# Three reorderings in a turn of a recurrent-attention and routed feed-forward kernel: products by u behind the row fetch, sums split the same way in every turn, one score copy moved

## The chip, the cores and the metric

The kernel runs on one core of one Trainium2 chip. A core has TensorE (PE, matrix products; its weight loads are listed as PEld), VectorE (DVE), ScalarE (ACT), GpSimd (POOL) and SyncE (SP, which issues most of the DMAs here). Each engine works through its own queue of instructions in order; engines wait for each other by semaphores. The metric is the device time of one execution in microseconds (us); less is better. Times of a kernel are medians of several runs.

## What is computed

The first part is a recurrent attention (RWKV6) over 4 batches, 8 heads, 768 positions and 48 values a head, with a state of 48 x 48 for each head:

```python
for t in range(S):
    cur = np.einsum('bhd,bhe->bhde', u[None] * kt, vt)
    y[:, :, t] = np.einsum('bhd,bhde->bhe', rt, state + cur)
    state = wt[:, :, :, None] * state + np.einsum('bhd,bhe->bhde', kt, vt)
```

The term of a position with itself, r . (u * k) times v, doesn't need the state: it is one number for each position and head, times v. The second part takes the result x (768 rows of 384 for each batch), scores each row, and puts the 128 best rows of a batch through a feed-forward block:

```python
scores = np.einsum('bsd,d->bs', x, w_gate)
for b in range(B):
    top_idx = np.argpartition(-scores[b], capacity)[:capacity]
    xe = x[b, top_idx]
    h = np.maximum(xe @ w1, 0.0)
    ye = h @ w2
    g = 1.0 / (1.0 + np.exp(-scores[b, top_idx]))
    out[b, top_idx] = x[b, top_idx] + g[:, None] * ye
```

All data is 32-bit; w1 is 384 x 1024, w2 is 1024 x 384.

## The kernel before

The 768 positions of a batch are cut into 6 chunks of 128, so there are 24 chunks. A chunk's attention is computed in matrix form: running products of the decays w (two scans on VectorE), r and k scaled by them (`R`, `K`), a masked score product, the product with v, and a state that is carried from chunk to chunk.

The order of the work is written out by hand. `turn(i)` is called for i from -2 to 24, and it works on several chunks at once, in different stages: the inputs of chunks i + 1 and i + 2 are transposed and scaled, the scores and outputs of chunk i are computed, the output rows of chunk i - 1 are turned back, written and scored, and the scores of chunk i - 2 are compared with those of its batch. The order in which `turn` calls the stages is the order of the instructions in each engine's queue. A later instruction of a queue can't overtake an earlier one that waits.

The stages that matter here, with their lines:

- **The term of a position with itself.** `own_products` (L367, GpSimd) multiplies r and k of chunk i + 1; `own_weights` (L370, GpSimd) multiplies that by u; one turn later `own_values` (L378, ScalarE) sums each of the 8 heads in an ACTIVATE with an accumulator, and `own_results` (L387, mostly GpSimd) multiplies v by the sums. `own_values` is called at two places of a turn: a first group of heads early, the rest after the rows of the chunk before have been copied. `FIRST` is 5 heads. From turn 9 on (`LATE` is 9) the first group is empty when no feed-forward work is waiting at that moment; this happens in turn 9 only.
- **State and rows.** `back` (L420, ScalarE copies `kt` out of a PSUM bank of a pool of two), `rows_back` (L470, ScalarE copies `x` out; in the last two turns L468 on VectorE), `rows_out` (L476 on GpSimd adds the term above, L477 on SP stores the rows), `row_products` (L481, GpSimd multiplies the rows by the gate weights into `scr`) and `row_sums` (L486, ScalarE sums `scr` to the scores). From turn 9 on `row_sums` stands ahead of the copies `yt` (L459) in ScalarE's queue; in turns up to 8 it stands behind the copy (L456).
- **Comparing scores.** `compared` transposes a chunk's scores on TensorE (L552, `ps_e`) and compares them on VectorE (L554 against the chunks before, L558 within the chunk); `kept` (L568, ScalarE) copies the transposed scores into `every` for the chunks that follow. `kept` can run only when L558 is done.
- **Choosing rows.** When a batch's 6 chunks are scored, `mixture` runs as a generator through the turns that follow: ranks (L587 on TensorE, L594 and L595 on VectorE), six picks (L605, VectorE, 16-bit), an index product (L614 on TensorE) and `idx` (L620, VectorE), and the fetch of the chosen rows by an indirect DMA from GpSimd's queue (L629); a turn later the rows are transposed (L638, `ps_x`) and copied to `xeT` (L640, ScalarE). Each `mix(place=...)` in `turn` runs the generator on by one piece if that piece belongs there. The picks of the first batch come at the end of turn 7, its fetch in turn 8; for the second and third batch picks and fetch are in turns 14 and 20; the last batch's are after the last turn.
- **Feed-forward.** `forward` is a generator too: 8 groups of 3 products (L674, `ps_h`), with a copy `hid` (L679, ScalarE) after each 4 groups, then 8 products (L686, `ps_f`), then the gated result (L693) and a scattered store (L696). `fed_in_turn` runs a few pieces of it at two places of a turn.

Of the kernel before, what the change touches and what calls it, by code (L numbers as in the profile page):

```python
# [37 lines left out]
def kernel(  # L38
# [43 lines left out]
    B, H, S, D = r.shape  # L82
# [11 lines left out]
    LATE = S // L + 3  # L94

    FIRST = H * 5 // 8
# [21 lines left out]
    N = len(chunks)  # L118
# [43 lines left out]
    def loads(n):  # L162
        load(v_bufs, v, n - 3)
        load(k_bufs, k, n - 1)
        load(r_bufs, r, n - 1)
        load(w_bufs, w, n)
# [19 lines left out]
    def load_weights(n):  # L186
        while n > 0 and weights:
            to, src = weights.pop(0)
            nc.sync.dma_start(out=to, in_=src)
            n -= 1  # L190
# [67 lines left out]
    def warm(n):  # L258

        ps = psM.tile([L, 512], FP32, tag="m", name="ps_n")  # L260
        for _ in range(n):
            nc.tensor.matmul(
                ps, nothing.to_broadcast([L, L]), nothing.to_broadcast([L, 512]),
                start=True, stop=True,
            )

    def spread(to, row):

        ps = psM.tile([L, C], FP32, tag="m", name="ps_b")
        nc.tensor.matmul(ps, one_row, row, start=True, stop=True)  # L270
        nc.scalar.copy(out=to, in_=ps)
# [46 lines left out]
    def check_sums():  # L318

        above = setup.tile([L, 1], FP32)  # L320
        nc.vector.tensor_reduce(out=above, in_=guard, axis=AX.X, op=ALU.add)
        below = setup.tile([L, 1], FP32)
        junk = setup.tile([L, N * HP], FP32)
        nc.vector.tensor_scalar(
            out=junk, in0=alls.rearrange("p n j -> p (n j)"), scalar1=float(LOW ** L),
            scalar2=None, op0=ALU.is_lt, op1=ALU.add, accum_out=below,
        )
        return above, below
# [377 lines left out]
    mixing, picked, feed, ended, sums = [], [], [], [], []  # L706

    def step(f, n, *more):
        if 0 <= n < N:
            f(work.setdefault(n, dict(n=n)), *more)  # L710

    def mix(n=1, place=None):


        while n > 0 and mixing:
            if place is not None and mixing[0][1] not in (None, place):
                return
            try:
                mixing[0][1] = next(mixing[0][0])
                n -= 1  # L720
            except StopIteration:
                mixing.pop(0)

    def fed(n, on=True):

        while n > 0:
            if not feed:
                if not picked:
                    return
                feed.append((picked[0][0], forward(*picked.pop(0))))  # L730
            try:
                last = next(feed[0][1])
                n -= 1
                if last and not on:
                    return
            except StopIteration:
                feed.pop(0)

    def fed_in_turn(n, few):

        kept = (feed or picked) and (feed or picked)[0][0] == B - 2
        fed(few if kept else n, on=False)
# [6 lines left out]
    def turn(i):  # L749
        soon = i >= N - 1  # L750
        step(first_left, i + 1)
        if i < 1:
            step(scaled_aside, i + 1, "K", "right")
        step(own_products, i + 1)
        if i <= LATE:
            step(scores, i)

        first = FIRST if i < LATE or feed or picked else 0
        step(own_values, i, range(first))
        step(carry, i - 1, work.get(i))  # L760
        if i > 0:
            step(scaled, i + 1, "K", "right")
        mix(place="picks")
        if i >= 0:
            step(own_weights, i + 1)
        if soon:
            step(masked, i)
        if i == N - 1:
            sums.extend(check_sums())
        if i < N:  # L770
            step(compared, i - 2)
        if i < LATE:
            step(kept, i - 2)
        step(back, i)
        if LATE <= i < N:
            step(kept, i - 2)
        step(rows_back, i - 1, soon)
        mix(place="half")
        if not soon:
            step(masked, i)  # L780
        step(rows_out, i - 1, soon)
        step(row_scores_soon if soon else row_products, i - 1)
        step(own_values, i, range(first, H))
        step(own_results, i)
        fed_in_turn(PIECES // 2, 2 if i >= N - 1 else 1)
        mix(place="sum")
        step(inputs_t, i + 1, "R", r_bufs)
        if i == -1:
            spread(wg_bc, wg_row)
        step(scaled, i + 1, "R", "left")  # L790
        step(decays_t, i + 2)
        mix(place="mid")
        if i == -2:
            warm(2)
        step(range_check, i + 2)
        if i >= LATE and not soon:
            step(row_sums, i - 1)
        if i == -1:
            spread(u_bc.rearrange("p h d -> p (h d)"), u_row)
            step(own_weights, i + 1)  # L800
        step(carry_products, i)
        step(outputs_t, i)
        if i >= LATE:
            step(scores, i + 1)
        step(inputs_t, i + 2, "K", k_bufs)
        if i == -2:
            warm(1)
        if 0 <= i - 2 < N - 1 and chunks[i - 2][1] == NCH - 1:
            mixing.append([mixture(chunks[i - 2][0]), "ranks"])
        mix(place="ranks")  # L810
        fed_in_turn(PIECES - PIECES // 2, 1 if i == N - 1 else 0)
        if i == N - 1:
            step(compared, i - 1)
            step(kept, i - 1)
        if i < LATE and not soon:
            step(row_sums, i - 1)
        step(scans, i + 2)
        if i < LATE:
            mix(place="picks")
        mix(place="end")  # L820
        if i > -2:
            loads(i + 5)
        if i in WEIGHT_TURNS:
            load_weights(1)

    with tc.manual_schedule():
        warm(6)
        for i in range(-2, N + 1):
            turn(i)

        ended.append(True)
        mix(1000)
        mixing.append([mixture(B - 1), "picks"])
        step(compared, N - 1)
        step(kept, N - 1)
        fed(1)
        mix(2)
        wide = checked(sums)
        fed(1)
        mix()  # L840
        fed(NFC - 2)
        mix(2)
        fed(2)
        mix(1000)
        fed(1000)
        outside = nc.values_load(wide, min_val=0, max_val=1)
# [73 lines left out]
```

## Time and profile before

| | |
|---|---|
| median of 3 runs | 200.09 us (199.82 to 200.36) |
| the profiled execution's own time | 199.46 us |
| its span, first to last instruction | 197.8 us |
| mean granted TensorE clock | 0.995 |
| sums of own values, L378, ScalarE | 192 ACTIVATEs of 241 ns, each with an accumulator read of 197 ns |
| product by u, L370, GpSimd | 24 of 1002 ns |
| product by gate weights, L481, GpSimd | 22 of 1004 ns |
| picks, L605, VectorE | 24 of 301 ns (240 to 1036) |
| copy of scores, L568, ScalarE | 20 of 267 ns |
| fetch of rows, L629, GpSimd | 4 of 1096 ns; 3.3 us from issue to landing |

How to read the profile: in a list of groups each line gives source line, engine, operation, output and inputs, shapes and count, then busy time, mean duration and the idle time of the engine just before, with what ended it. An ACTIVATE and its accumulator read overlap, so the eight sums of a chunk follow each other every 0.23 us. A line of the list of waits gives the engine and line that waited, what it waited for, and the us in total, the times and the longest. In a timeline each line is: start, duration, engine, line, operation, and in brackets the idle time before it. The chain of waits is followed back from the last instruction; a wait on several semaphores is put down to the one that came last. Turn 8 lies at about 57 to 64 us, turn 9 at 64 to 72, turn 14 at 101 to 108, turn 20 at 144 to 152, turn 23 at 166 to 170, and the feed-forward of the last batch ends the span.

### The profile page before, as it was taken

What the parts mean: (1) busy time and instruction counts of PE and PEld (TensorE: products, weight loads), DVE (VectorE), ACT (ScalarE), POOL (GpSimd) and SP (SyncE); (2) the same over time, 40 slices, a digit from 0 to 9 for tenths busy, and PEclk for the clock granted to TensorE, in tenths of its full rate; (3) what the DMA queues carried; (4) which work ended last, traced back from release to release, by engine and by line L of the source; (5) the groups of instructions that cost most, each with busy time, mean ns of one, the idle gap of its engine ahead of it and who ended that gap; (6) DMA issues with size and microseconds to landing.
All of it is one profiled execution on the core that took longest, in us unless ns stands there. A gap on an engine that the chain in (4) does not pass through costs nothing.

```text
span 197.8 us, 7207 instructions
## 1 busy us (share of the span) xinstructions
PE 183.4 (93%) x2674; PEld 149.9 (76%) x2675; DVE 160.3 (81%) x348; ACT 129.4 (65%) x668; POOL 139.4 (70%) x186
## 2 busy tenths in 40 slices
PE   7898999989799989999999999999999999899970
PEld 3477787867686779898788798897878798777830
DVE  6999899999999978998989888999989886751010
ACT  4588999998974777669556768777666766410300
POOL 8699899995886995587658799579649796122201
PEclk9999999999999999999999999999999999999998
DMA  7999999989999999999894796897954131111101
GB/s 111 164 163 152 172 197 173 254 172 161 224 204 252 222 193 243 226 219 197 160 207 104 145 206 129 110 180 138 150 100 122 46 77 45 40 45 41 40 8 45
DMA packets 105390, 28.86 MB, mean 146 GB/s; under 512 B 100482, under 2 KB 104580, under 8 KB 105348
## 3 DMA queue, kind: packets, MB, share of 16 engines
q1 hardware_dynamic: 104304, 26.65, 74.7%
q0 software_dynamic: 512, 1.57, 2.6%
q8 instruction: 23, 0.38, 0.9%
q14 instruction: 19, 0.16, 0.3%
q10 hardware_dynamic: 532, 0.10, 0.3%
HBM read 22.81 MB, written 5.51 MB: 143 GB/s over the span
## 4 chain that ended last, share of the span: by engine, by line
PE 65%; ACT 11%; DMA 8%; SPq 5%; DVE 5%; issue 2%; POOL 0%; POOLq 0%; DVEq 0%
PE ps_h L674 11%; PE ps_f L686 11%; PE ps_s L402 9%; PE ps_t L277 7%; SPq L157 5%; PE ps_t L284 5%; PE ps_kv L507 4%; PE ps_yt_y L442 4%; PE ps_yt_y L450 3%; PE ps_w L277 3%; DMA v_buf<-in_v_dram 3%; PE ps_yt_k L442 3%; DMA k_buf<-in_k_dram 3%; ACT rk L378 3%; DMA r_buf<-in_r_dram 2%; ACT vo L391 2%
## 5 line engine op out<-in xcount | busy, mean ns | idle before, releaser
L378 ACT ACTIVATE rk<-rk 128x48 f32<-128x48 f32 x192 | 44.4, 241 | 0.1
L378 ACT ACTIVATION_READ_ACCUMULATOR rk<-rk 128x1 f32 x192 | 37.8, 197 | 0.0
L476 POOL TENSOR_TENSOR x<-x,vo 128x384 f32<-128x384 f32 x22 | 22.1, 1005 | 17.3 <-ACT x L470 17.1
L308 DVE TENSOR_TENSOR_SCAN left<-ps_w,from_left 128x511 f32<-128x511 f32 x24 | 30.7, 1281 | 0.9
L410 DVE TENSOR_TENSOR sc<-ps_s,before_f 128x1024 f32<-128x1024 f32 x24 | 29.2, 1218 | 1.4 <-PE ps_s L402 1.4
L297 DVE TENSOR_TENSOR_SCAN right_buf<-ps_w,from_right 128x511 f32<-128x511 f32 x24 | 29.1, 1211 | 1.0 <-PE ps_w L277 1.0
L402 PE MATMUL ps_s<-R,K 64*64 64x128 f32 x768 | 25.9, 272 | 1.7 <-ACT yt L456 0.9
L674 PE MATMUL ps_h<-xeT,w 128*128 128x128 f32 x192 | 25.0, 278 | 1.2 <-ACT hid L679 1.2
L674 PEld LDWEIGHTS ps_h<-xeT,w 128*128 128x128 f32 x192 | 22.9, 192 | 2.4 <-ACT hid L679 1.9
L370 POOL TENSOR_TENSOR rk<-rk,u_bc 128x384 f32<-128x384 f32 x24 | 24.1, 1002 | 1.0 <-DVE alls L303 0.5
L402 PEld LDWEIGHTS ps_s<-R,K 64*64 64x64 f32 x768 | 21.4, 133 | 4.1 <-ACT yt L456 3.3
L367 POOL TENSOR_TENSOR rk<-r_buf,k_buf 128x384 f32<-128x384 f32 x24 | 24.1, 1006 | 0.5 <-DMA r_buf<-in_r_dram 0.4
L686 PE MATMUL ps_f<-w,hid 128*128 128x384 f32 x64 | 23.5, 495 | 0.0
L481 POOL TENSOR_TENSOR scr<-x,wg_bc 128x384 f32<-128x384 f32 x22 | 22.1, 1004 | 1.7
L387 POOL TENSOR_TENSOR vo<-v_buf,own 128x384 f32<-128x384 f32 (+1 forms) x24 | 17.7, 737 | 3.4 <-ACT rk L378 3.4
L420 ACT COPY kt<-ps_t 128x384 f32<-128x384 f32 x20 | 9.6, 480 | 15.4 <-PE ps_t L284 15.3
L355 DVE TENSOR_TENSOR R<-ps_t,left 128x512 f32<-128x512 f32 x24 | 16.4, 685 | 3.1 <-issue 2.2
L486 ACT ACTIVATE scr<-scr 128x384 f32<-128x384 f32 x22 | 11.5, 525 | 9.9 <-POOL scr L481 9.7
L355 DVE TENSOR_TENSOR K<-ps_t,right_buf 128x512 f32<-128x512 f32 x22 | 15.0, 682 | 2.6 <-PE ps_t L277 1.9
L277 PE MATMUL ps_t<-ident,k_buf 128*128 128x128 f32 x96 | 15.7, 286 | 0.2 <-DMA k_buf<-in_k_dram 0.2
L277 PE MATMUL ps_t<-ident,r_buf 128*128 128x128 f32 x96 | 14.7, 275 | 1.1 <-DVE K L355 0.4
L277 PE MATMUL ps_w<-ident,w_buf 128*128 128x128 f32 x96 | 15.1, 281 | 0.6 <-ACT every L568 0.4
(131 smaller groups left out, 404.7 us busy)
## 6 DMA issues: line engine op xcount, KB each, us to landing
k_buf<-in_k_dram SPq DMA_DIRECT2D x24, 192.0 KB, 5.3
r_buf<-in_r_dram SPq DMA_DIRECT2D x24, 192.0 KB, 5.4
v_buf<-in_v_dram SPq DMA_DIRECT2D x24, 192.0 KB, 4.3
out_dram<-x SPq DMA_DIRECT2D x24, 192.0 KB, 3.8
w_buf<-in_w_dram SPq DMA_DIRECT2D x23, 192.0 KB, 4.5
w<-in_moe_w_dram SPq DMA_DIRECT2D x3, 512.0 KB, 5.7
w<-in_moe_w_dram SPq DMA_DIRECT2D x4, 384.0 KB, 5.5
w_buf<-in_w_dram ACTq DMA_DIRECT2D x1, 96.0 KB, 3.4
```

The source lines that it names most:

```text
L277: nc.tensor.transpose(ps[:, j, :], src(j), ident)
L297: nc.vector.tensor_tensor_scan(out=flat[:, W - 2::-1], data0=wt[:, W - 1:0:-1], data1=from_right.rearrange("p j t -> p (j t)")[:, W - 2::- ...
L308: nc.vector.tensor_tensor_scan(out=left.rearrange("p j t -> p (j t)")[:, 1:W], data0=wt[:, 0:W - 1], data1=start.rearrange("p j t -> p (j ...
L355: nc.vector.tensor_mul(out, t.pop(name + "t"), t.pop(by))
L367: nc.gpsimd.tensor_mul(rk, r_bufs[n % NBUF][:, :, 0:D], k_bufs[n % NBUF][:, :, 0:D])
L370: nc.gpsimd.tensor_mul(t["rk"], t["rk"], u_bc)
L378: nc.scalar.activation(out=rk[:, h, :], in_=rk[:, h, :], func=AF.Copy, accum_out=o[:, h:h + 1])
L402: nc.tensor.matmul(ps[half(c), q, j, :], t["K"][half(q), j, half(c)], t["R"][half(q), j, :], start=True, stop=True,)
L410: nc.vector.tensor_mul(t["sc"].rearrange("p q j t -> p (q j) t"), ps.rearrange("p q j t -> p (q j) t"), _heads(before_f, 2 * HP),)
L476: nc.gpsimd.tensor_add(x, x, t.pop("vo").rearrange("p h d -> p (h d)"))
L674: nc.tensor.matmul(ps[:, q, :], w1[:, dc, (f0 + q) * L:(f0 + q + 1) * L], xeT[:, dc, :], start=(dc == 0), stop=(dc == NDC - 1),)
L686: nc.tensor.matmul(ps, hid[:, fc, :], w2[:, fc, :], start=(fc == 0), stop=(fc == NFC - 1))
```

## The change

Only the order of calls in `turn` is changed; no instruction is added or removed.

- The early group of `own_values` is five heads in every turn (before, it was empty in turn 9).
- `own_weights` for the next chunk is called behind `mix(place="half")`, that is, behind the fetch on GpSimd in the turns that have one (8, 14 and 20), instead of behind `mix(place="picks")`. In the other turns nothing on GpSimd lies between the two places.
- In turn 23 (i == N - 1, the first of those called `soon`) `kept` of chunk 21 is called behind `own_results` and the first feed-forward piece, instead of behind `back`. On ScalarE this puts the copy behind the last three sums and behind `hid`. In turn 24 `kept` isn't called at this place, before or after.

```diff
-        first = FIRST if i < LATE or feed or picked else 0
-        step(own_values, i, range(first))
+        step(own_values, i, range(FIRST))
         step(carry, i - 1, work.get(i))
         if i > 0:
             step(scaled, i + 1, "K", "right")
         mix(place="picks")
-        if i >= 0:
-            step(own_weights, i + 1)
         if soon:
             step(masked, i)
...
-        if i < LATE:
+        if i < LATE and not soon:
             step(kept, i - 2)
         step(back, i)
-        if LATE <= i < N:
+        if i >= LATE and not soon:
             step(kept, i - 2)
         step(rows_back, i - 1, soon)
         mix(place="half")
+
+        if i >= 0:
+            step(own_weights, i + 1)
         if not soon:
             step(masked, i)
         step(rows_out, i - 1, soon)
         step(row_scores_soon if soon else row_products, i - 1)
-        step(own_values, i, range(first, H))
+        step(own_values, i, range(FIRST, H))
         step(own_results, i)
         fed_in_turn(PIECES // 2, 2 if i >= N - 1 else 1)
+        if i == N - 1:
+            step(kept, i - 2)
         mix(place="sum")
```

The functions called are unchanged.

## The prediction

> **What bounds the kernel now.** I read the page first, then the chain of waits in order of time, then the waits of the stretches that the diff touches, and last the timeline of the engines concerned. The page's engine shares, and the shares of the chain that ended last:
>
> ```profile
> PE 183.4 (93%) x2674; PEld 149.9 (76%) x2675; DVE 160.3 (81%) x348; ACT 129.4 (65%) x668; POOL 139.4 (70%) x186
> ...
> PE 65%; ACT 11%; DMA 8%; SPq 5%; DVE 5%; issue 2%; POOL 0%; POOLq 0%; DVEq 0%
> ```
>
> TensorE is the bound nearly everywhere; GpSimd holds none of the chain. So an edit on the other engines pays only where the chain leaves TensorE. The chain in order of time (start, us, what) shows two such places that the diff touches:
>
> ```profile
> 58.02 2.12 DVE pick L605 x6
> 60.13 0.61 DVE K L355
> 60.79 0.57 PE ps_t L277 x4
> ...
> 67.30 0.48 ACT x L470
> 67.78 0.93 ACT rk L378 x9
> 68.71 0.87 ACT rk L378 x7
> 69.58 0.37 ACT xeT L640
> 70.00 0.44 PE ps_yt_y L442 x4
> ...
> 168.95 0.68 ACT rk L378 x6
> 169.63 0.49 ACT hid L679
> 170.17 0.94 PE ps_h L674 x6
> ```
>
> From 72 to 166 us the chain is TensorE almost without a gap. (It also runs through input DMAs before 67.30; the copy there starts back to back on ScalarE, so I don't believe that link.) The waits in 57 to 72 us (turns 8 and 9), then in 166 to 172 us (turn 23):
>
> ```profile
> ACT kt L420 <- PE ps_t L284: 1.1, 1, 1.1
> ...
> PE ps_yt_y L442 <- ACT xeT L640: 0.9, 1, 0.9
> ```
>
> ```profile
> ACT every L568 <- DVE ahead L558: 2.3, 2, 1.3
> ...
> PE ps_h L674 <- ACT hid L679: 0.8, 1, 0.8
> ```
>
> TensorE stands 0.86 us (timeline) for the copy `xeT`, because eight sums L378 precede it, while ScalarE stood 1.07 us idle just before `kt`. In turn 23 it stands 0.84 us for `hid`, queued behind a copy `every` that waits 1.29 us for VectorE. Then the timeline of VectorE, GpSimd and ScalarE around the fetches:
>
> ```profile
> 58.02 2.12 DVE L605 TENSOR_SCALAR pick<-slots,rank 128x128 bf16<-128x128 bf16 x6
> 58.60 0.99 POOL L370 TENSOR_TENSOR rk<-rk,u_bc 128x384 f32<-128x384 f32 x1
> ...
> 61.42 1.24 POOL L629 DMA_INDIRECT xe<-out_dram,idx  x1 [1.83 <-DVE idx L620]
> ...
> 107.66 0.52 ACT L486 ACTIVATE scr<-scr 128x384 f32<-128x384 f32 x1 [1.91 <-POOL scr L481]
> ...
> 110.92 0.48 ACT L420 COPY kt<-ps_t 128x384 f32<-128x384 f32 x1 [0.89 <-PE ps_t L284]
> ```
>
> The six picks take 2.12 us in turn 8, but 1.21 in turns 14 and 20 and 1.07 in the tail. One of the six alone took 1036 ns (median 243), and it lies over L370. The fetch waits for `idx`, not for L370.
>
> **What the Trainium skill says.** "SBUF — State Buffer", section "Who interferes with whom": VectorE and GpSimd share one port pair as an exclusive lock; a VectorE instruction in a two-port mode and a GpSimd instruction block each other for the whole instruction. "VectorE: DVE Perf Modes", section "What auto-detection actually checks": a single source and destination of 16 bits in SBUF get the mode that uses both ports; that is the pick. The trace agrees: the pick beside L370 took 1036 ns, the one beside L527 505, those beside nothing 242. "Perfetto Trace Analysis", section "GPSIMD Engine Instruction", says to take GpSimd times from start-to-start spacing, so I use 0.96 us for L370 (66.96 to 67.92), not its 1.00.
>
> **The change part by part.** The order of instructions on TensorE, VectorE and SP is unchanged. On GpSimd only three pairs swap (L370 behind L629, turns 8, 14, 20); elsewhere nothing lies between the two places. On ScalarE the sums split as 5 + 3 in turn 9 alone, and one copy moves in turn 23.
>
> *Turn 8.* The third pick falls from 1036 to 242 ns: -0.79. `K` follows (end 60.73 to 59.94), the transposes of r (TensorE stood 0.42 us for `K`), `idx`, `sc`, `yt`: TensorE is 0.8 ahead at about 64. On GpSimd the fetch starts at 60.63, L370 follows (+0.96), so the row product `scr` ends at 64.91 against 64.78: 0.13 later than before, not 0.8 earlier. ScalarE's row sum L486 waits for it and ends near 65.55; TensorE's score transpose L552 waits for that (65.73 against 65.86). Most of the lead is gone here: -0.14.
>
> *Turn 9.* The five sums follow L316, 65.56 to 66.70 (5 x 0.228). `kt` was ready to start at 66.42 and starts at 66.70 against 66.58: the idle time of 1.07 covers nearly all of the sums, 0.12 shows. The r transposes need `kt`'s bank (67.24 against 67.12). Behind the copies only three sums are left (67.63 to 68.31). `ps_x` ends at 68.6, so `xeT` starts at 68.66 against 69.48, and TensorE's L442 at 69.2 against 70.00: **-0.80**. What is late next is TensorE itself: ps_kv ends at 69.2. GpSimd's `scr` of turn 9 ends at 70.13, its row sum at 70.8, just before `yt` can start (70.9). So of the two gains (0.79 and 0.86) the added GpSimd time swallows about one. Bounds: -0.3 if `scr` or `kt` is 0.5 later than I put them; -1.2 if the score isn't in the way. The TensorE-bound turns carry the lead on; inputs k and r of a chunk are issued about two turns ahead of use and land in 5.3 us, so I see no DMA that eats it.
>
> *Turns 14 and 20.* The fetch keeps its time: `idx` waits for TensorE's `ps_i`. The first pick loses its 0.14 of blocking, which nothing waits for. L370 now stands ahead of L476, L481 and L387: `scr` 0.95 late (107.63 to 108.58), so on ScalarE the row sum, both `yt` copies, L316 and five sums are 0.95 late, and `kt`, which waited 0.89 (0.87 in turn 20), starts up to 0.08 late. SP's output store and the loads of v, k, r, w queued behind it go 0.96 later too, with landing margins of microseconds; GpSimd itself recovers in its next idle time (1.22 and 1.21 us before L476). Cost 0.00 to 0.10 each, taken 0.05: **+0.10**. If the cover were gone it would be 0.95 each. Where L370 now lies, VectorE runs `R` and a scan, each with one operand in PSUM, so no new blocking: 0.
>
> *Turn 23.* ScalarE runs all eight sums in one piece, 166.15 to 167.97; `ps_h` ended at 167.63, so `hid` runs to 168.56. The copy still waits until 168.69 and delays nothing (`yt` can't start before 169.35). TensorE's second half L674 follows L450 at 169.33 instead of 170.17: -0.84. But the two score rounds behind it pass through VectorE: the second L558 starts at 170.59, when L554 ends, instead of 171.25; x L468, score L494 and the third L552 move by the same 0.66, and so do ranks, picks, fetch and the last feed-forward, an unbroken chain. **-0.66**, bounds -0.84 and -0.3.
>
> Sum: -0.80 + 0.10 - 0.66 = -1.36. The profiled execution took 199.46 us (span 197.8 and 1.66 around it), giving 198.10. It lies 0.63 below the median of 200.09; the same difference from the median gives **198.7 us**.
>
> **The rivals.** Differences within 0.3% (0.6 us) can't be told from none with this kernel.
>
> *Turns 8 and 9 give nothing:* the port lock stays busy, or the late row product on GpSimd holds ScalarE another 0.7 us. For it: 0.65 of the 0.79 is already lost at the score. Against: the 0.86 us that `xeT` costs has its own cause, eight sums ahead of it. -0.56: 199.5.
>
> *The moved copy gives nothing:* the lead of `hid` is lost in the next wait on VectorE. For it: L558 waits there 0.65 us for a transpose. Against: that wait is itself on TensorE, behind `ps_h`. -0.70: 199.4.
>
> *Slower: GpSimd's late row product, in turns 14 and 20.* The two-microsecond waits of ScalarE for L481 stand in front of `yt` and `kt`. If TensorE reaches the transposes for `kt` earlier than it did, the cover of 0.89 shrinks and the 0.95 shows. With turn 8 at +0.16 (0.95 against 0.79) and no gain in turn 9, it costs 0.16 + 1.90 - 0.66 = +1.40: 201.5. It turns the result when each of the two turns loses over 0.25, that is with a cover under 0.70. Against: both covers were measured, 0.89 and 0.87.
>
> *More than forecast:* the score isn't in the way in turn 8, and turn 23 gives 0.84: -1.2 + 0.1 - 0.84 = -1.94: 198.15.
>
> **How the numbers follow.** Chances: forecast 0.57; turns 8 and 9 nothing 0.13; the copy nothing 0.10; more 0.10; slower 0.10. The forecast's own range is 198.3 to 199.2 from its bounds; taking in the two half-gains, and leaving out the slower case and the lower part of the larger gain, the range is 198.2 to 199.8. Faster by over 0.3% (below 199.49): the forecast, the larger gain, the second rival and a third of the first, 0.81; within 0.3%: 0.10; slower: 0.09.
>
> **What would show it.** Right: six picks in about 1.3 us in turn 8; no wait of L442 for `xeT` over 0.2 in turn 9; ScalarE's wait for L481 in turns 14 and 20 near 2.9 us with `kt` after it hardly waiting; no wait of L674 for `hid` near 168 to 170, and the fetch of the last batch 1.3 us earlier (175.2). Wrong: `kt` late and TensorE waiting for it in turns 9, 15 or 21, or input loads late after 72 us.

## The result and the profile after

| | before | after |
|---|---|---|
| median of 4 runs each, taken together | 199.95 us (199.81 to 200.36) | 198.05 us (197.33 to 198.45) |
| the profiled execution's own time | 199.46 us | 197.93 us |
| its span | 197.8 us | 196.2 us |

The changed kernel is faster by 1.90 us: the ratio is 0.9897, with an interval of [0.9864, 0.9931]. The forecast was 198.7 us with a range of 198.2 to 199.8, so the direction was right and the time lies 0.15 us below the range. The two profiled executions differ by 1.53 us.

The page of the changed kernel, first the shares of the engines, then those of the chain that ended last, then two groups with the idle time ahead of them, and last the row sums on the page of before:

```profile
PE 183.9 (94%) x2675; PEld 150.5 (77%) x2675; DVE 159.1 (81%) x348; ACT 129.5 (66%) x668; POOL 139.3 (71%) x186
...
PE 70%; ACT 14%; DVE 5%; DMA 3%; issue 3%; POOL 2%; POOLq 0%
...
L674 PE MATMUL ps_h<-xeT,w 128*128 128x128 f32 x192 | 25.0, 278 | 0.4 <-ACT hid L679 0.4
L486 ACT ACTIVATE scr<-scr 128x384 f32<-128x384 f32 x22 | 11.6, 525 | 13.3 <-POOL scr L481 13.3
```

```profile
L486 ACT ACTIVATE scr<-scr 128x384 f32<-128x384 f32 x22 | 11.5, 525 | 9.9 <-POOL scr L481 9.7
```

The busy times are those of before (VectorE 1.2 us less, which is the blocked time of the picks), so the gain is idle time. TensorE's share of the chain grew from 65% to 70%. It now waits only 0.4 us for `hid` in the whole run, in place of 1.2. The row sums on ScalarE wait 13.3 us for GpSimd's row products, in place of 9.7: that is where the moved product shows, with about 0.95 us more in each of the turns 8, 14 and 20.

The timeline of the changed kernel, at the places that the prediction named (start, duration, engine, line, operation, idle time before):

```profile
58.05 1.09 DVE L605 TENSOR_SCALAR pick<-slots,rank 128x128 bf16<-128x128 bf16 x6
...
61.70 1.01 POOL L370 TENSOR_TENSOR rk<-rk,u_bc 128x384 f32<-128x384 f32 x1
...
64.78 0.52 ACT L486 ACTIVATE scr<-scr 128x384 f32<-128x384 f32 x1 [1.04 <-POOL scr L481]
...
65.45 0.32 PE L552 MATMUL ps_e<-ident,score 128*128 128x128 f32 x1 [0.55 <-ACT scr L486]
...
66.52 0.46 ACT L420 COPY kt<-ps_t 128x384 f32<-128x384 f32 x1
...
67.03 0.66 PE L277 MATMUL ps_t<-ident,r_buf 128*128 128x128 f32 x4 [0.49 <-ACT kt L420]
...
69.02 0.44 PE L442 MATMUL ps_yt_y<-sc,v_buf 128*64 128x128 f32 x4
...
107.63 0.52 ACT L486 ACTIVATE scr<-scr 128x384 f32<-128x384 f32 x1 [2.86 <-POOL scr L481]
...
109.94 0.48 ACT L420 COPY kt<-ps_t 128x384 f32<-128x384 f32 x1
...
168.72 0.94 PE L674 MATMUL ps_h<-xeT,w 128*128 128x128 f32 x6
```

Read it from the top. The picks take 1.09 us in place of 2.12. TensorE's wait of 0.86 for `xeT` ahead of L442 is gone. But TensorE has got two new waits, 0.55 for the row sum (L552, which needs the late row product) and 0.49 for `kt` (L277). In turn 14 the row sum stood idle 2.86 us where it stood 1.91, and `kt`, which had waited 0.89, starts with no wait. In turn 23 TensorE's L674 starts with no wait for `hid`.

Starts of the same TensorE work in both traces show how the lead comes and goes (us; the first row is the end of `K` on VectorE):

```
                                   before    after    after - before
K done, turn 8                      60.73    59.73        -1.00
score transpose L552, turn 9        65.86    65.45        -0.41
first transposes of r, L277         67.12    67.03        -0.09
products with v, L442, turn 9       70.00    69.02        -0.98
transposes of r, turn 15           111.45   110.47        -0.98
scores L402, turn 16               122.25   121.50        -0.75
scores L402, turn 22               165.25   164.72        -0.53
last feed-forward products, L686   186.34   184.90        -1.44
```

The lead of the picks, a whole microsecond, is nearly gone at the first transposes of r in turn 9; the five early sums then give 0.89 of their own. Nothing is lost in turns 14 and 15. Some 0.45 is lost between turns 15 and 22, at two places that no part of the change touches. Turn 23 and what hangs on it give 0.91.

### The profile page after: what moved, and what is told of

Its sections match the earlier page's. It is cut to its first block, busy times and chain, and to the rows that moved or that the text cites. A ratio compares the mean times of both kernels' runs of the same rounds, so it can differ in the third digit from the quotient of the medians.

```text
span 196.2 us, 7209 instructions
## 1 busy us (share of the span) xinstructions
PE 183.9 (94%) x2675; PEld 150.5 (77%) x2675; DVE 159.1 (81%) x348; ACT 129.5 (66%) x668; POOL 139.3 (71%) x186
## 4 chain that ended last, share of the span: by engine, by line
PE 70%; ACT 14%; DVE 5%; DMA 3%; issue 3%; POOL 2%; POOLq 0%
PE ps_h L674 11%; PE ps_s L402 10%; PE ps_f L686 9%; PE ps_t L277 8%; PE ps_t L284 5%; PE ps_kv L507 4%; ACT rk L378 4%; PE ps_yt_y L442 4%; PE ps_w L277 3%; DMA k_buf<-in_k_dram 3%; PE ps_yt_y L450 3%; PE ps_yt_k L442 3%; PE ps_yt L442 2%; ACT vo L391 2%; PE ps_e L552 2%
## 5 line engine op out<-in xcount | busy, mean ns | idle before, releaser
L297 DVE TENSOR_TENSOR_SCAN right_buf<-ps_w,from_right 128x511 f32<-128x511 f32 x24 | 29.1, 1211 | 1.0 <-PE ps_w L277 1.0
L402 PE MATMUL ps_s<-R,K 64*64 64x128 f32 x768 | 26.0, 272 | 1.7 <-ACT yt L456 0.9
L674 PE MATMUL ps_h<-xeT,w 128*128 128x128 f32 x192 | 25.0, 278 | 0.4 <-ACT hid L679 0.4
L370 POOL TENSOR_TENSOR rk<-rk,u_bc 128x384 f32<-128x384 f32 x24 | 24.1, 1006 | 1.2 <-ACT u_bc L271 0.7
L402 PEld LDWEIGHTS ps_s<-R,K 64*64 64x64 f32 x768 | 21.5, 133 | 4.1 <-ACT yt L456 3.3
L674 PEld LDWEIGHTS ps_h<-xeT,w 128*128 128x128 f32 x192 | 22.9, 192 | 1.5 <-ACT hid L679 0.8
L486 ACT ACTIVATE scr<-scr 128x384 f32<-128x384 f32 x22 | 11.6, 525 | 13.3 <-POOL scr L481 13.3
L277 PE MATMUL ps_t<-ident,k_buf 128*128 128x128 f32 x96 | 16.4, 292 | 0.0
L277 PE MATMUL ps_w<-ident,w_buf 128*128 128x128 f32 x96 | 15.2, 282 | 0.5 <-ACT every L568 0.4
L277 PE MATMUL ps_t<-ident,r_buf 128*128 128x128 f32 x96 | 14.7, 275 | 0.9 <-ACT kt L420 0.9
```

Of the source, the lines that this page charges most:

```text
L277: nc.tensor.transpose(ps[:, j, :], src(j), ident)
L297: nc.vector.tensor_tensor_scan(out=flat[:, W - 2::-1], data0=wt[:, W - 1:0:-1], data1=from_right.rearrange("p j t -> p (j t)")[:, W - 2::- ...
L370: nc.gpsimd.tensor_mul(t["rk"], t["rk"], u_bc)
L402: nc.tensor.matmul(ps[half(c), q, j, :], t["K"][half(q), j, half(c)], t["R"][half(q), j, :], start=True, stop=True,)
L674: nc.tensor.matmul(ps[:, q, :], w1[:, dc, (f0 + q) * L:(f0 + q + 1) * L], xeT[:, dc, :], start=(dc == 0), stop=(dc == NDC - 1),)
```

## The experiments

Three theories stood against each other. *The forecast:* the early sums and the moved copy carry the gain, and the product behind the fetch gives shorter picks and takes the time back through the late row product. *A rival:* the shorter picks are the gain, and the sums only shift it. *Another rival:* the copy gives little, since its lead is lost in the score rounds. I call the early sums in turn 9 A, the product behind the fetch B, and the moved copy C.

### Each part alone, and all but B

A alone keeps, of the diff shown, only this:

```diff
-        first = FIRST if i < LATE or feed or picked else 0
-        step(own_values, i, range(first))
+        step(own_values, i, range(FIRST))
...
-        step(own_values, i, range(first, H))
+        step(own_values, i, range(FIRST, H))
```

> Only the first part: five sums of own values ahead of the copies in turn 9; product by u and score copy as before. Theory (three places, each on the chain by itself): the sums fill the 1.07 us in which ScalarE stood idle before the copy of kt, kt isn't late (66.6 us), TensorE's wait of 0.86 us for xeT goes and TensorE's first product L442 of turn 9 starts at about 69.15 us instead of 70.00: 0.85 us faster than before. Rival (the lead is lost again in the TensorE-bound turns or in the loads): L442 earlier, but the end is not, 0 to 0.3 us faster.

B alone keeps only this:

```diff
         mix(place="picks")
-        if i >= 0:
-            step(own_weights, i + 1)
...
         mix(place="half")
+        if i >= 0:
+            step(own_weights, i + 1)
```

> Only the second part: product by u behind the fetch in turns 8, 14 and 20. Theory: the six picks of turn 8 take about 1.1 us instead of 2.12, VectorE is about 1 us ahead, but GpSimd's row product ends where it did (64.8 us) and the score of chunk 7 waits for it, so TensorE's L442 of turn 9 gains only 0.4 us; turns 14 and 20 show ScalarE waiting 2.9 us for the row product instead of 1.9 and lose under 0.1 each: 0.2 to 0.4 us faster than before. Rival (port lock worth its full length): 1.0 us faster. Rival (late row product decides in turns 14 and 20): slower than before.

C alone keeps only this:

```diff
-        if i < LATE:
+        if i < LATE and not soon:
             step(kept, i - 2)
         step(back, i)
-        if LATE <= i < N:
+        if i >= LATE and not soon:
             step(kept, i - 2)
...
         fed_in_turn(PIECES // 2, 2 if i >= N - 1 else 1)
+        if i == N - 1:
+            step(kept, i - 2)
```

> Only the third part: the score copy of chunk 21 behind the feed-forward piece in turn 23. Theory: TensorE doesn't wait for hid (0.84 us before) and everything behind it moves by the same amount up to the end: 0.85 us faster than before. Rival (my forecast's step: the score rounds on VectorE keep 0.2 of it back): 0.66 us. Rival (lost in the next wait): 0 to 0.2 us.

The fourth kernel has the edits of A and C without that of B.

> First and third part, without the second. Theory: the first two parts overlap in turns 8 and 9, since GpSimd's late row product takes back most of what the shorter picks give; without the second part turns 8 and 9 still gain 0.85 of the 0.98 us seen in the trace, so this kernel is 1.7 us faster than before and only 0.1 to 0.2 us slower than the changed kernel. Rival (parts add up): 1.3 to 1.5 us faster, and the changed kernel 0.4 us or more ahead of it.

Measured, all beside the same runs of the kernel before (median 199.46 us):

| kernel | median | ratio and interval | us |
|---|---|---|---|
| A alone | 198.78 | 0.9967 [0.995, 0.9983] | -0.68 |
| B alone | 199.05 | 0.9983 [0.9971, 0.9994] | -0.41 |
| C alone | 198.57 | 0.9959 [0.9943, 0.9974] | -0.89 |
| A and C, no B | 197.67 | 0.9906 [0.9888, 0.9925] | -1.79 |

The rival with the picks falls: without B the kernel has about the gain of the whole change (-1.90 in the first runs; runs of both side by side follow below). A's 0.68 is less than the 0.85 expected of it; its interval (0.34 to 1.00) includes both. The timeline of B alone tells why its shorter picks are worth so little:

```profile
58.05 1.07 DVE L605 TENSOR_SCALAR pick<-slots,rank 128x128 bf16<-128x128 bf16 x6
...
64.76 0.52 ACT L486 ACTIVATE scr<-scr 128x384 f32<-128x384 f32 x1 [1.04 <-POOL scr L481]
...
65.43 0.32 PE L552 MATMUL ps_e<-ident,score 128*128 128x128 f32 x1 [0.55 <-ACT scr L486]
...
69.41 0.33 PE L442 MATMUL ps_yt_y<-sc,v_buf 128*64 128x128 f32 x2 [0.68 <-ACT xeT L640]
```

The picks are 1.05 us shorter, but TensorE stops 0.55 for the row sum and then still 0.68 for `xeT`, whose eight sums are ahead of it as before. L442 starts at 69.41 in place of 70.00: 0.59 is left of 1.05. In the timeline of A alone the same stretch reads:

```profile
57.87 2.01 DVE L605 TENSOR_SCALAR pick<-slots,rank 128x128 bf16<-128x128 bf16 x6
...
64.55 0.52 ACT L486 ACTIVATE scr<-scr 128x384 f32<-128x384 f32 x1
...
66.33 0.48 ACT L420 COPY kt<-ps_t 128x384 f32<-128x384 f32 x1
...
68.32 0.48 ACT L640 COPY xeT<-ps_x 128x384 f32<-128x384 f32 x1
...
68.85 0.44 PE L442 MATMUL ps_yt_y<-sc,v_buf 128*64 128x128 f32 x4
```

The picks are still blocked. `kt` starts without a wait (the sums have filled the 1.07 us it used to stand idle), and `xeT` is no longer late. From the start of the picks to L442 it is 10.98 us, against 11.98 before (58.02 to 70.00) and 11.36 in B alone. So A gives 1.00 (0.11 of it is the picks' own difference), B 0.62. The whole change has 10.97 (58.05 to 69.02): together they give no more than A alone. In both the row sum L486 starts 6.7 us after the picks do (at 64.55 and 64.78) and `kt` 8.5 us after them (at 66.33 and 66.52): ahead of GpSimd's row product A alone has the blocked picks, and the whole change has the product by u, of about the same length.

C alone, VectorE, ScalarE and TensorE in turn 23:

```profile
167.97 0.58 ACT L679 ACTIVATE hid<-ps_h 128x512 f32<-128x512 f32 x1
...
168.69 0.27 ACT L568 COPY every<-ps_e 128x128 f32<-128x128 f32 x1
...
169.26 0.94 PE L674 MATMUL ps_h<-xeT,w 128*128 128x128 f32 x6
...
170.53 0.35 DVE L558 SCALAR_TENSOR_TENSOR ahead<-ps_e,score,after_f 128x128 bf16<-128x128 f32 x1
...
170.80 0.55 DVE L468 TENSOR_TENSOR x<-ps_t,vo 128x384 f32<-128x384 f32 x1
```

In the trace of before the same work is:

```profile
168.69 0.27 ACT L568 COPY every<-ps_e 128x128 f32<-128x128 f32 x1 [1.29 <-DVE ahead L558]
...
169.53 0.58 ACT L679 ACTIVATE hid<-ps_h 128x512 f32<-128x512 f32 x1
...
170.17 0.94 PE L674 MATMUL ps_h<-xeT,w 128*128 128x128 f32 x6 [0.84 <-ACT hid L679]
...
171.05 0.55 PE L284 MATMUL ps_t<-turned,yt 112*128 112x112 f32 x4
...
171.25 0.35 DVE L558 SCALAR_TENSOR_TENSOR ahead<-ps_e,score,after_f 128x128 bf16<-128x128 f32 x1 [0.65 <-PE ps_e L552]
...
171.69 0.56 DVE L468 TENSOR_TENSOR x<-ps_t,vo 128x384 f32<-128x384 f32 x1
```

The copy itself runs at the same 168.69; only what stood behind it has moved. `hid` is 1.56 earlier, L674 0.91, L558 0.72 and L468 0.89. So the score rounds take back nothing that lasts: from the scores of turn 22 to the last feed-forward products it is 20.19 us in C alone against 21.09 before (165.25 to 185.44 and to 186.34), 0.90 less, and the timed gain was 0.89. The rival that the copy gives little falls too.

### B in turn 8 alone, and B behind the row product

What would B cost in turns 14 and 20, and can the lead lost in turn 8 be kept? Three kernels beside one set of runs of the kernel before (median 199.0 us): the whole change again, the whole change with B in turn 8 only, and the whole change with the product in turn 8 one place further back, behind the row product that the score waits for. First the whole change:

> The changed kernel once more, in more rounds. Theory: the sum of what its trace shows against the trace of before (0.98 us in turns 8 and 9, about 0.87 in turn 23, some 0.2 lost in turns 15 and 21), 1.5 to 1.9 us faster than before. Rival: the 1.9 us between the medians was mostly scatter and the forecast's 1.36 us is right.

B in turn 8 only (turn 8 is `NCH + 2`), against the changed kernel:

```diff
         mix(place="picks")
+        if i >= 0 and i != NCH + 2:
+            step(own_weights, i + 1)
...
         mix(place="half")
-        if i >= 0:
+        if i == NCH + 2:
             step(own_weights, i + 1)
```

> The changed kernel, with the product by u behind the fetch in turn 8 only; in turns 14 and 20 it stays ahead of the fetch as before. Theory: in those turns kt waits for TensorE anyway, so the moved product costs nothing: same time as the changed kernel within 0.1 us, with ScalarE's wait for the row product back at 1.9 us there; the 0.2 us that TensorE lost after turn 15 and after turn 21 in the changed kernel's trace are not from it and come and go. Rival (the moved product is what those 0.2 us come from): 0.4 us faster than the changed kernel, and no such loss in the trace.

The product behind the row product in turn 8, against the changed kernel:

```diff
+        late = i == NCH + 2
-        if i >= 0:
+        if i >= 0 and not late:
             step(own_weights, i + 1)
...
         step(row_scores_soon if soon else row_products, i - 1)
+        if late:
+            step(own_weights, i + 1)
```

> The changed kernel, with the product by u of turn 8 put behind the row product on GpSimd instead of directly behind the fetch (turns 14 and 20 as changed). Theory (the lead of the shorter picks is lost at the score of chunk 7, which waits for the late row product): the row product of turn 8 ends at about 63.8 us instead of 64.7, TensorE's score transpose of turn 9 no longer waits 0.55 us, kt starts at about 66.0, and TensorE's L442 of turn 9 starts 0.5 us earlier than in the changed kernel: 0.5 us faster than it. Rival (the five sums or another wait hold kt): same time as the changed kernel.

| kernel | median | ratio and interval | us |
|---|---|---|---|
| the whole change | 197.53 | 0.9927 [0.9908, 0.9946] | -1.47 |
| B in turn 8 only | 197.46 | 0.9926 [0.9907, 0.9945] | -1.54 |
| product behind the row product in turn 8 | 196.84 | 0.9896 [0.9877, 0.9915] | -2.16 |

The 1.47 us of the whole change lie between its expectation and the rival's 1.36, and the interval (1.07 to 1.83) includes both.

B in turns 14 and 20 costs nothing that can be told: the two kernels are 0.07 us apart, and neither has the losses after turns 15 and 21 in this set, so the moved product isn't what makes them. In the kernel with B in turn 8 only, ScalarE in turn 14 waits as it did before the change:

```profile
106.27 0.52 ACT L486 ACTIVATE scr<-scr 128x384 f32<-128x384 f32 x1 [1.91 <-POOL scr L481]
...
109.52 0.48 ACT L420 COPY kt<-ps_t 128x384 f32<-128x384 f32 x1 [0.88 <-PE ps_t L284]
```

With the product there the idle time is 2.86 and the wait of `kt` is gone (the fence of the changed kernel above): 0.95 is moved into a cover of 0.88, and TensorE doesn't see it.

The last kernel is the fastest. Its timeline in turns 8 and 9:

```profile
62.77 1.00 POOL L481 TENSOR_TENSOR scr<-x,wg_bc 128x384 f32<-128x384 f32 x1
...
63.73 1.00 POOL L370 TENSOR_TENSOR rk<-rk,u_bc 128x384 f32<-128x384 f32 x1
63.81 0.52 ACT L486 ACTIVATE scr<-scr 128x384 f32<-128x384 f32 x1
...
64.76 0.24 ACT L378 ACTIVATE rk<-rk 128x48 f32<-128x48 f32 x1 [0.26 <-POOL rk L370]
...
64.86 0.29 PE L552 MATMUL ps_e<-ident,score 128*128 128x128 f32 x1
...
65.91 0.46 ACT L420 COPY kt<-ps_t 128x384 f32<-128x384 f32 x1
...
68.41 0.44 PE L442 MATMUL ps_yt_y<-sc,v_buf 128*64 128x128 f32 x4
```

The row product runs first and the row sum is 0.97 earlier than in the changed kernel (63.81 against 64.78). TensorE's score transpose has no wait. Now the sums wait 0.26 for the product by u, a smaller price. From the picks to L442 it is 10.35 us, against 10.97 in the changed kernel with picks of the same length: 0.62. Against the whole change in the same set of runs the timed gain was 0.69, and the runs of the two don't overlap (196.72 to 197.08 us against 197.38 to 197.77).

### Repeats, and the early sums taken out of the best version

> First and third part without the second, now on one chip with the whole change. Theory (beside the five sums the product by u behind the fetch gives nothing, since the late row product takes back what the picks give): within 0.2 us of the whole change, 1.7 us faster than before. Rival (the second part has its own share): 0.3 us or more slower than the whole change.

> The whole change once more, beside the version without its second part. Theory: 0.9 us from turns 8 and 9 and 0.92 from turn 23, 1.8 us faster than before. Rival (the forecast's sum): 1.36 us.

> Product by u behind the row product in turn 8, on the same chip as the whole change. Theory: 0.6 to 0.7 us faster than the whole change (L442 of turn 9 starts 10.35 us after the picks instead of 10.97 to 11.10). Rival: the 0.69 us between medians of one call were scatter, 0 to 0.3 us.

The fourth kernel is the version with the product behind the row product, the best so far, without A:

```diff
-        step(own_values, i, range(FIRST))
+        first = FIRST if i < LATE or feed or picked else 0
+        step(own_values, i, range(first))
...
-        step(own_values, i, range(FIRST, H))
+        step(own_values, i, range(first, H))
```

> The same as the run before, but with the eight sums of turn 9 behind the copies again. Theory (sums ahead of xeT and late row product are two separate holds of turn 9): kt near 7.6 us after the start of the picks, TensorE waits again for xeT and L442 starts about 11.0 us after the picks instead of 10.35; 0.6 to 0.7 us slower than the run before, about as fast as the whole change. Rival (the sums don't matter once the row product is early): same as the run before.

Measured beside one set of runs of before (median 199.58 us):

| kernel | median | ratio and interval | us |
|---|---|---|---|
| A and C, no B | 197.86 | 0.9894 [0.9875, 0.9913] | -1.72 |
| the whole change | 197.95 | 0.992 [0.9897, 0.9942] | -1.63 |
| product behind the row product in turn 8 | 197.33 | 0.9883 [0.9868, 0.9898] | -2.25 |
| the same without A | 198.45 | 0.9938 [0.9913, 0.9962] | -1.13 |

Side by side the whole change is no faster than A and C without B. Their traces agree: from the picks to L442 it is 11.14 us in the first trace of A and C (11.65 in the second, whose loads landed late), and 10.97, 11.10 and 11.19 in the three of the whole change. As in the set before, the gain of the whole change lies between the expected 1.8 and the forecast's 1.36, and its interval (1.16 to 2.06) includes both. Twice the best version is ahead of the whole change, by 0.69 and 0.62 us, and here too the runs don't overlap (197.14 to 197.44 against 197.55 to 199.02). Without A it has the wait again that A had removed; its timeline:

```profile
71.61 0.44 PE L442 MATMUL ps_yt_y<-sc,v_buf 128*64 128x128 f32 x4 [0.86 <-ACT xeT L640]
```

From the score transpose to L442 it is 4.14 us there (67.47 to 71.61), as before (65.86 to 70.00), and 3.56 with A. That is the 0.6 us expected. The start of `kt` and of L442, counted from the picks, missed what was expected: 8.09 and 11.51 us in place of 7.6 and 11.0. In this execution loads landed late (the last section), and TensorE's scores of turn 8 (L402) start 0.31 us before the picks in place of 0.98, so that the picks are no common mark. Counted from those scores, L442 starts after 11.82 us, against 11.32 in the best version, 11.95 in the changed kernel and 12.92 before. The timed difference of 1.1 us is uncertain in size: the runs without A spread from 197.57 to 200.33, all above those of the best version, and the profiled one was the slowest of them.

## Why the prediction came out as it did

Turns 8 and 9 and turn 23 moved the way that the forecast described, and turns 14 and 20 stayed within its bounds. Two of its steps failed by their size: the 0.63 us added to get from a profiled execution to a median, and the term of turn 23, -0.66, which measured -0.91. With the 0.63 the forecast was 198.73 us before rounding, and the median was 198.05. Of these 0.68 us, 0.51 come from the added distance, which was 0.12 for the changed kernel, and 0.17 from the sum.

**Turns 8 and 9, forecast -0.80: right, and step by step.** Three traces of the whole change gain 1.01, 0.88 and 0.79 us from the picks to L442. The third is the one to lay beside the forecast, since in it, as in the trace of before, a pick of about 500 ns is left, which the forecast didn't touch. Its timeline:

```profile
58.04 1.32 DVE L605 TENSOR_SCALAR pick<-slots,rank 128x128 bf16<-128x128 bf16 x6
...
66.73 0.45 ACT L420 COPY kt<-ps_t 128x384 f32<-128x384 f32 x1
67.24 0.66 PE L277 MATMUL ps_t<-ident,r_buf 128*128 128x128 f32 x4 [0.49 <-ACT kt L420]
...
69.23 0.44 PE L442 MATMUL ps_yt_y<-sc,v_buf 128*64 128x128 f32 x4
```

The forecast had picks of about 1.3 us, `kt` at 66.70, the transposes of r at 67.24 and L442 at 69.2. From picks to L442 this run gains 0.79.

What the other two gain beyond that isn't forced by the change. The forecast left the block of a pick by L527 (505 ns) where it was. Whether it occurs depends on when L527 runs. The list of the six picks of turn 8 (shortest, median and longest, ns), in the trace of before, then in the first, the second and the third trace of the whole change:

```profile
L605 DVE TENSOR_SCALAR pick<-slots,rank x6: 242/248/1036, 58.0 to 59.9; 128x128 bf16<-128x128 bf16 x6
```

```profile
L605 DVE TENSOR_SCALAR pick<-slots,rank x6: 240/242/277, 58.0 to 58.9; 128x128 bf16<-128x128 bf16 x6
```

```profile
L605 DVE TENSOR_SCALAR pick<-slots,rank x6: 238/240/411, 58.1 to 59.0; 128x128 bf16<-128x128 bf16 x6
```

```profile
L605 DVE TENSOR_SCALAR pick<-slots,rank x6: 241/245/500, 58.0 to 59.1; 128x128 bf16<-128x128 bf16 x6
```

L370's block of 1036 is gone in all three. L527's is nearly gone in the first, and the longest pick (277, 411, 500) differs between them as the gain does (1.01, 0.88, 0.79). GpSimd's timeline says why, first of the first trace, then of the third:

```profile
56.13 1.00 POOL L367 TENSOR_TENSOR rk<-r_buf,k_buf 128x384 f32<-128x384 f32 x1
...
57.77 0.51 POOL L527 TENSOR_TENSOR state<-mid,alls 128x192 f32<-128x192 f32 x1
```

```profile
56.63 1.00 POOL L367 TENSOR_TENSOR rk<-r_buf,k_buf 128x384 f32<-128x384 f32 x1 [0.55 <-DMA r_buf<-in_r_dram]
...
58.26 0.56 POOL L527 TENSOR_TENSOR state<-mid,alls 128x192 f32<-128x192 f32 x1
```

Where r lands 0.5 us later, L527 is pushed over the picks, which start at 58.05 and 58.04. The Trainium skill ("SBUF — State Buffer", section "Who interferes with whom") says that whoever issues first has the shared ports for the whole instruction; both traces agree: in the first L527 has run for 0.28 us when the picks start and ends within the first of them, which takes 277 ns, and in the third it starts among the picks and one of them takes 500 ns.

**Turns 14 and 20, forecast +0.10: nothing.** I took 0.05 each, the middle of bounds from 0 to 0.10. The covers (0.89 and 0.87, against a product of 0.96) were just enough: the lead of 0.98 is the same on both sides of turn 14, and the kernel with B in turn 8 alone ran like the whole change. The moved product blocks nothing on VectorE there, as forecast: in turn 14 `R` and the scan L297 take 0.68 and 1.21 us before and after.

**Turn 23, forecast -0.66: the term that was too small.** It is -0.91 in the changed kernel (20.18 us from those scores to those products, against 21.09) and -0.90 in C alone. The forecast stopped `hid`'s lead of 0.84 at VectorE, where L558 can't start before L554 ends. That much held: L558 was 0.72 earlier. The mistake was to move L468 by the same amount. Before, it followed L558's start by 0.44 us, and I carried that spacing on. Part of it was a wait: the four transposes L284 into `ps_t`, which L468 reads, ended on TensorE at 171.60, right before it started at 171.69 (the trace of before, in the section on C). With TensorE 0.91 earlier the spacing is 0.27, so L468 gains 0.89, all that TensorE gave. My upper bound of 0.84, TensorE's own wait, was too low for the same stretch, since its lead measured 0.91.

**The base.** The sum of -1.36 was right for the profiled execution to within 0.17 (198.10 forecast, 197.93 measured). I then added 0.63, the distance of the profile of before from its median of three. That step failed, as the distance didn't carry over: the changed kernel's profiled execution lies 0.12 below its own median. In three further sets the median of before was 199.46, 199.0 and 199.58, so 200.09 was a high base. Without the added 0.63 the forecast would have lain 0.05 from the median of 198.05. The range failed here, since its bounds covered the costs and not the scatter of the medians. As a ratio the forecast was 198.7 / 200.09 = 0.9931, inside the intervals of both repeats and at the edge of the first.

**Why the sum fitted the profile better than its terms.** In the traces the change is worth -0.98, 0 and -0.91, which is -1.89. Of that the changed kernel's trace gives back 0.45 between turns 15 and 22. All eight kernels of the first and third sets show a loss at the same two places, with and without each part; none of the second set does. Two kernels stand in both kinds: the whole change and the best version lose there in the third set and not in the second. So the loss isn't the change's; its cause stays open. The three terms gave 0.53 more than was forecast and met a loss of 0.45 that wasn't forecast. That the sum came within 0.17 of the profiled execution is luck.

**The rivals.** *Turns 8 and 9 give nothing* and *the copy gives nothing* were each contradicted by a part alone (A -0.68, C -0.89). *More than forecast* named the right size (198.15), and half of its reason: turn 23 gave more than forecast, but the score was in the way in turn 8. *The slower one* needed a cover under 0.70 in turns 14 and 20, and that didn't happen.

## What to carry to other kernels

When an instruction is moved to free another engine, follow what it now delays on its own queue: here a microsecond won on VectorE was lost at GpSimd's row product, and one place further back in the queue kept it. Take a spacing from an old trace only after asking whether it holds a wait that the change shortens too. Before adding a small gain to a median, find out how far medians of that size scatter, and widen the range by it.

## What the runs showed that I had not expected

The start of turn 8's picks varies from 57.41 to 60.10 us over the traces, though no kernel differs ahead of them; that is more than any part of the change. Eleven of the thirteen lie between 57.41 and 58.07, and the two late ones follow input loads that land late. The waits at 50 to 60 us in the trace of the best version without A, whose profiled execution was slow:

```profile
PE ps_kv L507 <- DMA v_buf<-in_v_dram: 1.9, 1, 1.9
...
POOL rk L367 <- DMA r_buf<-in_r_dram: 1.8, 1, 1.8
```

The repeat of A and C without B shows the same two waits (1.9 and 1.7 us) and a profiled time of 199.67 us, against a median of 197.86. One profiled execution of this kernel can thus lie 1.8 us above its median with nothing in the program to account for it.

The second surprise is the pair of pauses after turns 15 and 21: some 0.2 us each that TensorE loses among the four transposes of the next k (0.85 us in place of 0.66 after turn 15 in the changed kernel), while the trace names no releaser. From the scores of turn 15 to those of turn 16 it is 7.31 or 7.32 us in four traces (before, and the second set) and 7.38 to 7.61 in the nine others; from turn 21 to 22 it is 6.87 or 6.88 in the same four and 6.93 to 7.09 in the same nine. One and the same kernel has them in one set and not in another, and I haven't found what makes them. Medians of one kernel shift between the two sets by about as much: the whole change is 0.42 us slower in the third set than in the second, and the best version 0.49, while their traces lose 0.35 and 0.45 to the pauses. That the pauses make the shift isn't shown, but it is a reason to compare only kernels of one set.
